# Taking the norms of one attention batch through a power operation on GpSimd, pair by pair, with its squares on ScalarE

## The chip, the cores and the metric

The kernel runs on one core of one Trainium2 chip. Times are device microseconds (us) of that core, medians of several executions. All runs told here were in the fast state but two: one of six runs of the last experiment was slow and is left out of its median, and one single run of the kernel before, told as such, has no state. Names: TensorE multiplies matrices, VectorE, ScalarE and GpSimd do elementwise work, SyncE issues most DMAs. In profile lines they are PE, DVE, ACT, POOL and SP. In these traces each engine works through its instructions in one fixed order, that of the program: both profiles of the changed kernel have TensorE's 4161 matmuls in the same order.

## The reference

Cosine attention for 8 batches of 12 heads (448 tokens, 64 numbers per head), then a two-layer feed-forward with a quick GELU.

```python
q_n = q / (np.linalg.norm(q, axis=-1, keepdims=True) + 1e-06)
k_n = k / (np.linalg.norm(k, axis=-1, keepdims=True) + 1e-06)
scores = np.matmul(q_n, k_n.transpose(0, 1, 3, 2)) / tau     # then softmax, then @ v
# ...
h = x @ w_in
g = h * (1.0 / (1.0 + np.exp(-1.702 * h)))
return (g @ w_out).astype(np.float32)
```

## The kernel before

Heads are handled in pairs; pairs 0 to 5 are batch 0, 6 to 11 batch 1, and so on. A planner inside the program simulates the engines with fixed durations and writes the instructions of each engine in the order that comes out, so a change of a planned duration also changes orders. For each pair: load q, k and v; square; sum per head and token; make the inverse norm; scale q and k to fp16 ("qks"); transpose them ("tps", copied out as "qkT"); scores ("sp"), exponential ("et"), times values, normalise. When a batch's heads are done, its first feed-forward product begins ("mm" from w_in, then tanh "th" and gate "gT"), later the second (w_out).

```python
SQP, SQT, XA, CA = range(HP, 2 * HP), (0, 1), (), (0, 1)   # HP = 6: squares of pairs 6..11 on GpSimd
...
def square(x, ti):
    ...
    if sq_pool(x, ti):
        return nc.gpsimd.tensor_tensor(out=sqs[x, ti], in0=src, in1=src, op=ALU.mult)
    return nc.scalar.activation(out=sqs[x, ti], in_=src, func=AF.Square)
...
def newton(grp, ca, cb):                      # 3 VectorE instructions; called twice
    a, y, t = nrms[grp]
    nc.vector.scalar_tensor_tensor(out=t, in0=y, scalar=-ca, in1=y, op0=ALU.mult, op1=ALU.mult)
    nc.vector.tensor_tensor(out=t, in0=t, in1=a, op=ALU.mult)
    nc.vector.scalar_tensor_tensor(out=y, in0=t, scalar=cb, in1=y, op0=ALU.add, op1=ALU.mult)
...
def root(grp):                                # batch 0 only, before the first tanh
    nc.scalar.activation(out=a, in_=a, func=AF.Ln)
    nc.scalar.activation(out=a, in_=a, func=AF.Exp, scale=0.5)
...
groups = [(x,) for x in range(HP)]                                     # batch 0: one pair at a time
groups += [tuple(range(g, g + 2)) for g in range(HP, HALF, 2)]         # batch 1: in twos
groups += [tuple(range(g, g + GRP)) for g in range(HALF, NPAIR, GRP)]  # the rest: in threes
```

The three PSUM buffers of TensorE's products are given back mostly by VectorE (those of the w_out products by ScalarE): a product waits until VectorE's gate or copy has emptied the buffer it needs. TensorE also does filler transposes of a constant until 50 us, so as not to stand idle.

## Time and profile before

| | kernel before |
|---|---|
| time, median of 4 (with the run beside the changed kernel) | 445.4 us (444.07 to 446.61) |
| profiled span | 441.8 us |
| busy: TensorE, VectorE, ScalarE, GpSimd | 426.5, 240.6, 302.6, 146.2 us |
| first product of batch 1 starts | 99.18 us |
| loads of batch 2 resume | 74.21 us |

The span is shorter than the time of the run by some 2 us of start and end. A start time in the table is read from the timeline, the first line of that kind.

### The profile page before, as it was taken

The numbers are of one execution on the slowest core, as the hardware profiler recorded it, in microseconds if no ns is written. First come the engines' busy times: TensorE is split into PE (matmuls) and PEld (weight loads), VectorE is DVE, ScalarE is ACT, GpSimd is POOL, SyncE is SP. The second block draws the span as 40 slices with busy tenths as digits, with TensorE's granted clock in tenths as the row PEclk, the third lists the DMA queues.
The fourth block names the chain that finished last, engine by engine and source line by source line (L and its number), as shares of the span: only waits on it lengthen the run. The fifth ranks groups of instructions, "written<-read, shape, count | busy, mean of one in ns | idle before, by whom it ended". The sixth has DMA issues, their size and how long they took to land.

```text
span 441.8 us, 10584 instructions
## 1 busy us (share of the span) xinstructions
PE 426.5 (97%) x4174; PEld 262.6 (59%) x4174; DVE 240.6 (54%) x629; ACT 302.6 (69%) x478; POOL 146.2 (33%) x209
## 2 busy tenths in 40 slices
PE   8899989989999998999999999999999999999995
PEld 8768876554555654566555655555556655565563
DVE  4767987795877668653675338641552115404400
ACT  5889368959999878866887678865776466314411
POOL 2745767276436663324060613333000000000000
PEclk9999999999999999999999999999999999999999
DMA  9999298999999999666555766644311130021022
GB/s 222 242 226 264 69 163 173 244 245 281 217 218 204 230 248 187 178 132 173 173 131 114 209 182 130 158 103 127 54 26 46 50 96 13 12 73 36 1 72 73
DMA packets 95889, 64.00 MB, mean 145 GB/s; under 512 B 56288, under 2 KB 90848, under 8 KB 95840
## 3 DMA queue, kind: packets, MB, share of 16 engines
q1 hardware_dynamic: 91952, 56.81, 55.3%
q0 software_dynamic: 3648, 6.29, 8.0%
q8 instruction: 33, 0.54, 0.5%
q10 hardware_dynamic: 240, 0.23, 0.1%
q14 instruction: 16, 0.13, 0.1%
HBM read 45.61 MB, written 11.01 MB: 128 GB/s over the span
## 4 chain that ended last, share of the span: by engine, by line
PE 84%; DVE 5%; ACT 4%; DMA 2%; POOL 2%; issue 1%; SPq 0%; POOLq 0%; ACTq 0%
PE mm L557 31%; PE mm L502 28%; PE sp L377 7%; PE avp L403 7%; PE tps L348 4%; PE mm L532 2%; ACT et L388 2%; DMA k<-in_k_dram 2%; PE mm L456 2%; PE sp L439 2%; POOL qks L316 2%; PE tps L340 1%; DVE n L250 1%; ACT sq L244 1%; DVE gT L544 1%
## 5 line engine op out<-in xcount | busy, mean ns | idle before, releaser
L388 ACT ACTIVATE et<-sp 112x896 f16<-112x896 f32 x192 | 166.7, 917 | 39.8 <-PE sp L377 33.4
L557 PE MATMUL mm<-w_out,gT 128*128 128x384 f16 x896 | 154.8, 326 | 0.4 <-DVE xT L489 0.4
L502 PE MATMUL mm<-xT,w_in 128*128 128x448 f16 x672 | 135.4, 353 | 1.4 <-DVE gT L519 1.3
L557 PEld LDWEIGHTS <-gT 128*128 128x128 f16 x896 | 83.8, 98 | 65.5 <-issue 13.8
L502 PEld LDWEIGHTS <-w_in 128*128 128x128 f16 x672 | 62.3, 98 | 68.8 <-issue 15.6
L519 DVE SCALAR_TENSOR_TENSOR gT<-th,mm 128x448 f16<-128x448 f16 x112 | 68.8, 617 | 60.7 <-ACT th L512 60.7
L512 ACT ACTIVATE th<-mm 128x448 f16<-128x448 f32 x128 | 69.8, 548 | 39.5 <-PE mm L502 28.7
L250 DVE TENSOR_REDUCE n<-sq 112x8 f32<-112x512 f32 x96 | 63.6, 678 | 28.8 <-ACT sq L244 28.1
L332 POOL CAST vt<-v 112x256 f16<-112x256 f32 x92 | 35.0, 404 | 114.1 <-PE avp L403 73.6
L316 POOL TENSOR_TENSOR qks<-k,y 112x512 f16<-112x512 f32 x42 | 43.8, 1043 | 40.0 <-DVE y L291 33.0
L568 ACT ACTIVATE ost<-mm 128x384 f32<-128x384 f32 x56 | 27.5, 491 | 42.9 <-PE mm L557 41.1
L403 PEld LDWEIGHTS <-et 112*128 112x128 f16 x1152 | 44.7, 97 | 11.3
L414 DVE RECIPROCAL rcx<-avp 128x4 f32<-128x4 f32 x72 | 13.0, 180 | 62.9 <-PE avp L403 62.4
L403 PE MATMUL avp<-vt,et 112*128 112x65 f16 x1152 | 46.7, 193 | 0.0
L316 POOL TENSOR_TENSOR qks<-q,y 112x512 f16<-112x512 f32 x42 | 43.8, 1043 | 0.0
L377 PE MATMUL sp<-qkT 64*128 64x448 f16 x288 | 41.1, 355 | 0.0
L244 ACT ACTIVATE sq<-k 112x512 f32<-112x512 f32 x42 | 26.4, 633 | 8.9 <-DMA k<-in_k_dram 7.0
L417 DVE TENSOR_TENSOR xf<-avp,rcx 128x256 f16<-128x256 f32 x72 | 30.6, 424 | 2.5
L244 ACT ACTIVATE sq<-q 112x512 f32<-112x512 f32 x42 | 26.3, 633 | 0.8 <-DVE n L250 0.4
L348 PE MATMUL tps<-ident 128*128 128x128 f16 x254 | 19.4, 238 | 3.2 <-DVE qkT L352 1.8
L348 PEld LDWEIGHTS <-ident 128*128 128x128 f16 x254 | 17.3, 108 | 4.7 <-issue 3.3
L532 PE MATMUL mm<-xT,w_in 128*128 128x224 f16 x192 | 20.0, 259 | 0.1
(44 smaller groups left out, 217.3 us busy)
## 6 DMA issues: line engine op xcount, KB each, us to landing
k<-in_k_dram SPq DMA_DIRECT2D x48, 224.0 KB, 4.5
v<-in_v_dram SPq DMA_DIRECT2D x48, 224.0 KB, 4.5
q<-in_q_dram SPq DMA_DIRECT2D x47, 224.0 KB, 4.6
w_in<-in_moe_w_in_dram POOLq DMA_DIRECT2D x2, 1536.0 KB, 16.3
w_out<-in_moe_w_out_dram POOLq DMA_DIRECT2D x2, 1536.0 KB, 11.1
out_dram<-ost SPq DMA_DIRECT2D x7, 336.0 KB, 2.9
out_dram<-ost SPq DMA_DIRECT2D x8, 288.0 KB, 3.2
out_dram<-ost SPq DMA_DIRECT2D x8, 240.0 KB, 3.0
```

Source lines behind the costliest of these rows:

```text
L244: return nc.scalar.activation(out=sqs[x, ti], in_=src, func=AF.Square)
L250: nc.vector.tensor_reduce(out=n2s[grp][:, x - grp[0], ti], in_=sqs.pop((x, ti)), axis=AX.X, op=ALU.add,)
L316: return eng.tensor_tensor(out=qkss[x][:, 1 - ti].rearrange("p c j d -> p j c d"), in0=src, in1=rss[x][:, ti, :, :, None].to_broadcast((P, ...
L332: copy(out=vt[:, :, j, :D], in_=src[:, j]) for j in range(2)
L348: nc.tensor.transpose(out=tps0[:, 2 * S : 2 * S + 128], in_=ident, identity=ident)
L377: nc.tensor.matmul(out=sp[:, j, :S], lhsT=keys(x, j, c), rhs=queries(x, j, 0, S), start=True, stop=True,)
L388: nc.scalar.activation(out=e[:, : 2 * S].rearrange("p (j s) -> p j s", j=2), in_=sps.pop(key)[:P, :, :S], func=AF.Exp, scale=inv_tau, **kw,)
L403: nc.tensor.matmul(out=ps[:, (D + 1) * t : (D + 1) * (t + 1)], lhsT=exps[x, c][:, q0 : q0 + 128], rhs=values(x, c, D * j, D * j + D + 1), ...
L502: nc.tensor.matmul(out=ps[:, :S], lhsT=w_in_sb[:, kk, 128 * m : 128 * (m + 1)], rhs=xTs[b, kk][:, :S], start=(kk == 0), stop=(kk == KT1 - 1),)
L512: nc.scalar.activation(out=ths[key], in_=mms[key][:, :S], func=AF.Tanh, scale=0.851)
L519: nc.vector.scalar_tensor_tensor(out=gts[b // 2][:, m, (b % 2) * S : (b % 2 + 1) * S], in0=ths.pop((b, m)), scalar=1.0, in1=mms.pop((b, m) ...
L557: nc.tensor.matmul(out=mms[b2, t, n][:, :NW], lhsT=gts[b2][:, kk, 128 * t : 128 * (t + 1)], rhs=w_out_sb[:, kk, NW * n : NW * (n + 1)], st ...
```

## The change

The norms of batch 1 are freed from VectorE. Their square root becomes one power (exponent 0.5) per pair on GpSimd, the twelve squares move to ScalarE, and the w_out loads are planned earlier.

```diff
-    SQP, SQT, XA, CA = range(HP, 2 * HP), (0, 1), (), (0, 1)
+    SQP, SQT, XA, CA, TA, POW = (), (0, 1), (), (0, 1), (), range(HP, 2 * HP)
...
+    root_of = const.tile([P, 1], FP32)          # filled with 0.5
...
+    def power(grp):
+        a = n2s[grp]
+        flat = a.rearrange("p g a b c -> p (g a b c)")
+        return nc.gpsimd.tensor_tensor(
+            out=flat, in0=flat, in1=root_of.to_broadcast((P, 16 * len(grp))), op=ALU.pow
+        )
...
-    groups += [tuple(range(g, g + 2)) for g in range(HP, HALF, 2)]
+    groups += [tuple(range(g, g + 1)) for g in range(HP, HALF)]
...
+        if x == grp[0] and x in POW:
+            add(("norm", 0, grp), "POOL", 0.4 + 2.3 * n, early + 0.3, partial(power, grp), after=reds)
+            add(("norm", 1, grp), "DVE", 0.45, early + 0.3, partial(inverse, grp), after=[("norm", 0, grp)])
...
-        add(("w_out", i), "POOL", 1.0, 9 + i, partial(load_w_out, i), ...
+        add(("w_out", i), "POOL", 1.0, 3 + i, partial(load_w_out, i), ...
```

In the first lines `POW` names the pairs whose norm is a power; `TA` is empty and does nothing here. The function `inverse` (an add of 1e-6 and a reciprocal on VectorE) was there already for batch 0.

More of the change, by code (lines that the diff above doesn't have):

```diff
@@ L351, in transposed @@
         qkTs[x] = p_qkT.tile([128, 2, S], FP16, name="qkT")
-        nc.vector.tensor_copy(out=qkTs[x], in_=tpss.pop(x))
+        (nc.scalar.copy if x in TA else nc.vector.tensor_copy)(out=qkTs[x], in_=tpss.pop(x))
     def dma_transposed(x):
@@ L641 @@
                 add(("norm", 1, grp), "DVE", 0.45, early + 0.3, partial(inverse, grp), after=[("norm", 0, grp)])
-        if x == grp[0] and not first:
+        if x == grp[0] and x in POW:
+            add(("norm", 0, grp), "POOL", 0.4 + 2.3 * n, early + 0.3, partial(power, grp), after=reds)
+            add(("norm", 1, grp), "DVE", 0.45, early + 0.3, partial(inverse, grp), after=[("norm", 0, grp)])
+        elif x == grp[0] and not first:
             add(("norm", 0, grp), "DVE", 0.78 + 0.06 * n, early + 0.3, partial(norm_a, grp), after=reds, **port)
@@ L652 @@
                 after=[("scale", 0, x), ("scale", 1, x)], takes=[("a", 1), ("qkT", 1)], frees=[("qks", 2)])
-            add(("qkT", x), "DVE", 0.6, s - 3, partial(transposed, x), after=[("tp", x)], frees=[("a", 1)])
+            add(("qkT", x), "ACT" if x in TA else "DVE", 0.8 if x in TA else 0.6, s - 3, partial(transposed, x), after=[("tp", x)], frees=[("a", 1)])
         else:
@@ L770 @@
             dma=packets(768, 4096), **port)
-        add(("w_out", i), "POOL", 1.0, 9 + i, partial(load_w_out, i), hold=[("load", "q", 2 * HP - 1)],
+        add(("w_out", i), "POOL", 1.0, 3 + i, partial(load_w_out, i), hold=[("load", "q", 2 * HP - 1)],
             dma=packets(1024, 3072), **port)
@@ L775 @@
     make_identity(nc, ident)
+    nc.vector.memset(root_of, 0.5)
     for vt in vts:
```

## The prediction

> **What bounds the kernel now.** I read four views in this order: the page, the busy time of each engine in stretches of ten microseconds, the timelines of VectorE and GpSimd between 30 and 110 us, and the waits. The page first:
>
> ```profile
> PE 426.5 (97%) x4174; PEld 262.6 (59%) x4174; DVE 240.6 (54%) x629; ACT 302.6 (69%) x478; POOL 146.2 (33%) x209
> ...
> PE   8899989989999998999999999999999999999995
> ...
> DVE  4767987795877668653675338641552115404400
> ACT  5889368959999878866887678865776466314411
> POOL 2745767276436663324060613333000000000000
> ```
>
> TensorE is busy in 97% of the span and full in nearly every slice after the ninth (a slice is 11 us). VectorE and GpSimd, whose work the change moves, are full nowhere but between about 40 and 70 us. That is where batch 1 is prepared: its norms, its scaled queries and keys, and the first scores, beside the first feed-forward product of batch 0. The stretches show it:
>
> ```profile
> 30.00:40.00 10.00, 9.57 (x162) 8.01 (x161) 5.65 (x17) 9.30 (x13) 3.08 (x3) 1.00 1.11 260
> 40.00:50.00 10.00, 8.90 (x125) 8.35 (x125) 9.53 (x24) 5.12 (x8) 8.08 (x12) 1.00 0.78 184
> 50.00:60.00 10.00, 9.28 (x106) 9.03 (x104) 9.25 (x22) 4.35 (x8) 6.83 (x9) 1.00 0.51 81
> 60.00:70.00 10.00, 9.10 (x131) 6.44 (x132) 8.53 (x25) 8.04 (x10) 6.97 (x7) 1.00 1.05 178
> 70.00:80.00 10.00, 9.28 (x145) 6.08 (x143) 6.19 (x21) 8.37 (x12) 4.75 (x6) 1.00 0.77 178
> 80.00:90.00 10.00, 8.60 (x123) 5.29 (x119) 8.67 (x28) 9.88 (x16) 2.78 (x7) 1.00 1.10 243
> ```
>
> After the stretch come TensorE, its weight loads, VectorE, ScalarE, GpSimd, the clock, the DMA share and GB/s. From 40 to 60 us VectorE is at 94% while ScalarE idles half the time, because no score of batch 1 exists yet; from 80 us ScalarE is full of the exponentials that came late. The VectorE timeline shows Newton steps standing still:
>
> ```profile
> 44.66 1.04 DVE L276 SCALAR_TENSOR_TENSOR t<-y 112x32 f32<-112x32 f32 x1
> ...
> 56.59 2.15 DVE L263 TENSOR_SCALAR y<-n 112x32 int32<-112x32 int32 x1
> ```
>
> and the GpSimd timeline names what ran beside them:
>
> ```profile
> 44.61 1.04 POOL L243 TENSOR_TENSOR sq<-k 112x512 f32<-112x512 f32 x1
> ...
> 56.66 1.04 POOL L316 TENSOR_TENSOR qks<-k,y 112x512 f16<-112x512 f32 x1
> 57.66 1.03 POOL L316 TENSOR_TENSOR qks<-q,y 112x512 f16<-112x512 f32 x1
> ```
>
> The same L276 takes 0.18 us at 51.92 when GpSimd is not on a tensor. The Newton work of pairs 6 and 7 starts at 44.45 and ends at 53.38: 8.9 us for some 2 us of arithmetic.
>
> **What the Trainium skill says.** (1) "SBUF — State Buffer" calls the second port pair of VectorE, shared with GpSimd, an exclusive lock: a VectorE instruction in a two-port mode, or with two SBUF inputs against a GpSimd instruction that reads SBUF, waits until the other is done (its list of key terms, "shared port pair"). The trace agrees: 1.04 against 0.18 us above. (2) "GPSIMD Engine Reference", section "Performance versus the Vector engine", gives 2.6 cycles per element for an add on GpSimd and nothing for a power; no run so far shows one. (3) "ScalarE: Activation LUTs", section "Table sets: the hidden batching unit", says that exp and ln share one set and exp and tanh another, so a logarithm between tanh calls would cost a table load. The trace has two loads of 1.283 us, one at the start and one before the first tanh; the instruction order of the changed kernel also has two. So batch 1, which lies among the tanh calls, could not take batch 0's root by logarithm and exponential for free; Square causes no load.
>
> **The change part by part.** (a) Removed from VectorE: three groups of two pairs, eleven instructions each. From the groups by shape: L263 3.0, L276 2.0, L279 1.3, L280 1.3, L287 0.5, L290 1.1, L291 0.6, together 9.8 us, of which about 3 us is waiting for the port. (b) Added to VectorE: an add and a reciprocal for each of six pairs. Batch 0's rows of the same shape measure 319 and 253 ns, so 6 x 0.57 = 3.4 us. VectorE loses 6.4 us net in 40 to 73 us. (c) Moved: twelve squares leave GpSimd (12 x 1.04 = 12.5 us) and go to ScalarE (12 x 0.633 = 7.6 us), into the hole that ScalarE has from 40 to 60 us (10.5 us idle). (d) Added to GpSimd: six powers on 112x16. No row has one. The kernel's own plan enters 2.7 us for it; I take that, because its other GpSimd figures hold (a scale planned at 1.0, spaced 1.00 us in the timeline; a cast planned at 0.75, measured 0.75). So 6 x 2.7 = 16.2 us: GpSimd gains 3.7 us net. (e) The norms come pair by pair, so batch 1's first transposes come earlier. Counting both TensorE orders: they stand after 180 of the 192 first-product matmuls before, after 96 of 192 in the changed kernel. Thirteen of 254 filler transposes go as well. (f) The second half of the w_out load follows the first at once, instead of 9.0 us later (53.69 and 62.69 before).
>
> What can be gained at most? From the pieces of the chain, one matmul of L532 takes 0.096 us, L557 0.163, L456 0.037, L439 0.075, L340 and L479 0.05, L502 0.19. Times the counts of each stretch, real TensorE work is 8.1, 8.8, 8.7, 9.1, 8.2 and 10.0 us in the six stretches from 40 to 100 us: 53 of 60. So the change has 7 us to win there, 1.6% of the time. After 100 us TensorE idles for 1.3 us once and never again before the end.
>
> How much of the 7? Following the new GpSimd order by hand: ScalarE gives the second square of pair 6 at about 39, VectorE its sum at 39.9, the first power ends at 42.6. A pair then costs one power, two scales and a share of casts, 2.7 + 2.0 + 0.4 = 5.1 us; with the two w_out issues at about 52 to 54 us (1.9 us), the last pair is scaled at about 72.8 and transposed by 73.2. In the kernel before, the last transposes of batch 1 end at 77.2 and batch 1's own first product starts at 99.3, 22.1 us later. Behind that point the changed order holds 92 L557, 96 L456, 28 L439 and 14 L479 matmuls: 15.0 + 3.5 + 2.1 + 0.7 = 21.3 us; with 1.5 us of stalls (2.5 us before) the first product of batch 1 starts at 96.0. That is **3.3 us earlier**. From there the order is nearly the old one, so I carry the 3.3 us to the end.
>
> **The rivals.** *GpSimd becomes the pace.* The six pairs cost it 5.1 us each, as much as TensorE has to do meanwhile; nothing measured stands behind 2.7 us. If a power takes 4 us, six of them add 7.8 us and the gain turns into a loss of about 4 us; at 1.7 us TensorE is the bound and the gain nears 5.5. *The port.* A power may hold the port for its 2.7 us and stop the next pair's add on VectorE, and with it the gates behind it; five such collisions at up to 2.7 us would give VectorE back its 6.4 us and leave about 0 to 1 us. For it: the collisions shown above. Against: VectorE is below 90% after the change. *The loads.* The waits of the queues have one large entry:
>
> ```profile
> SPq L231 <- DMA w_out<-in_moe_w_out_dram: 32.0, 1, 32.0
> ```
>
> Batch 2's loads wait for w_out until 74.2 us, and ScalarE then waits for keys at 150 to 166 us. If the data come no earlier, TensorE just waits where it now waits 1.3 us. Issuing the second half early hides nothing by itself, since the DMA engines were busy without a break between the halves; only the earlier first half (about 1.7 us) counts. Under this rival the gain is 1 to 2 us.
>
> **Range and chances.** I take 3.3 us off 446.3 us: 443.0 us. The range goes from the 7 us ceiling (439.5) to a slow power (447.5). Over 2% faster would need 8.9 us, more than the ceiling of 7: 3%. Over 2% slower needs a power of about 5 us or a broken order: 5%. Within 2%: 92%.
>
> **What would show it.** Right: powers spaced near 2.7 us; VectorE 6 us less busy in all; ScalarE at 7 to 8 tenths between 40 and 60 us; the first scores of batch 1 near 49 us instead of 60.5; its first product near 96 us. Wrong: TensorE waiting at the batch 1 transposes for GpSimd by more than 4 us in all; adds on VectorE lasting over 1 us beside powers; the first product of batch 1 early but a larger wait for keys by 170 us.

## The result

The changed kernel takes 439.62 us (439.36 to 440.5, 4 runs) against 445.4 us. The ratio is 0.9874, with a 95% interval of 0.9837 to 0.9912. A second set gave 439.57 us against 444.25 us, ratio 0.9885 (0.9862 to 0.9909). A ratio is the mean time of one kernel's fast runs over that of the other's of the same rounds, so not quite the ratio of the medians quoted. Executions over 1.5% slower than the fastest of the same kernel are left out of the means. The interval shows a real gain of 1.2 to 1.3%, about 5 us.

First the page of the changed kernel, engine totals and tenths per slice of 11 us:

```profile
PE 425.0 (97%) x4161; PEld 260.2 (59%) x4161; DVE 238.3 (54%) x612; ACT 307.3 (70%) x490; POOL 151.2 (34%) x203
...
PE   8898999999999999999999999999999999999996
...
DVE  4866987785876768643775339641552115404400
ACT  5889977859999878776797578765776466314411
POOL 2752998276437564333060604343100000000000
```

VectorE lost only 2.3 us of busy time (the prediction said 6), GpSimd gained 5.0, ScalarE 4.7. From 44 to 77 us the digits of GpSimd now read 9, 9, 8 where they read 7, 6, 7. The stretches of ten microseconds, with the same columns as in the prediction:

```profile
40.00:50.00 10.00, 9.74 (x140) 8.47 (x137) 9.41 (x20) 9.93 (x18) 9.28 (x7) 1.00 1.08 232
50.00:60.00 10.00, 9.06 (x128) 6.84 (x124) 9.67 (x25) 7.76 (x12) 9.99 (x8) 1.00 0.60 94
60.00:70.00 10.00, 10.00 (x142) 8.39 (x138) 7.03 (x15) 7.92 (x13) 10.00 (x8) 1.00 1.16 211
70.00:80.00 10.00, 9.76 (x172) 6.84 (x168) 8.00 (x24) 8.85 (x13) 6.08 (x12) 1.00 0.61 161
80.00:90.00 10.00, 9.01 (x92) 5.32 (x89) 8.16 (x26) 8.06 (x14) 3.69 (x8) 1.00 1.11 266
```

ScalarE's hole from 40 to 60 us is mostly gone (9.93 and 7.76 us busy in ten) and its crush at 80 us has eased (9.88 to 8.06). GpSimd has no gap from 41 to 74 us. VectorE is still nearly full from 40 to 60 us. The moved squares have a price, too: one that waited for its keys holds up the first tanh behind it (37.50 us instead of 36.46), and TensorE waits 1.40 us for the gate after that, at 38.75 us. VectorE's group of adds shows why its total fell so little; this is the groups by shape, with count, busy time and mean in ns:

```profile
L315 DVE TENSOR_SCALAR yv<-n 112x16 f32<-112x16 f32 x12 | 7.4, 615 | 1.3 <-POOL n L308 1.1
```

Six of the twelve are batch 0's, which took 319 ns on average in the kernel before. In the timeline of VectorE the six of batch 1 take 0.36, 1.00, 0.96, 0.78, 1.05 and 1.01 us, 0.86 on average. The timelines of GpSimd and of VectorE around one power say what holds them:

```profile
45.35 2.90 POOL L308 TENSOR_TENSOR n<-n,root_of 112x16 f32<-112x16 f32 x1
48.22 1.04 POOL L325 TENSOR_TENSOR qks<-q,yv 112x512 f16<-112x512 f32 x1
```

```profile
48.29 1.00 DVE L315 TENSOR_SCALAR yv<-n 112x16 f32<-112x16 f32 x1
```

The power ends at 48.25. That releases both the add on VectorE and the next instruction on GpSimd, and GpSimd's scale starts 0.07 us sooner. It has the port for its whole 1.04 us, so the add lasts 1.00 us. The Trainium skill ("SBUF — State Buffer", section "Terms") calls the port an exclusive lock; these lines agree. The lock is lost to the scale behind the power, not to the power.

Two more lines of the timelines give the position of TensorE at the first product of batch 1, before and after:

```profile
99.18 1.30 PE L502 MATMUL mm<-xT,w_in 128*128 128x448 f16 x6
```

```profile
96.75 2.43 PE L511 MATMUL mm<-xT,w_in 128*128 128x448 f16 x12
```

### The profile page after: what moved, and what is told of

It is laid out like the page before. It is cut to its first block, busy times and chain, and to the rows that moved or that the text cites. A ratio compares the mean times of both kernels' runs of the same rounds, so it can differ in the third digit from the quotient of the medians.

```text
span 438.5 us, 10541 instructions
## 1 busy us (share of the span) xinstructions
PE 425.0 (97%) x4161; PEld 260.2 (59%) x4161; DVE 238.3 (54%) x612; ACT 307.3 (70%) x490; POOL 151.2 (34%) x203
## 4 chain that ended last, share of the span: by engine, by line
PE 82%; POOL 5%; issue 4%; DVE 4%; DMA 2%; ACT 1%; SPq 0%; POOLq 0%; ACTq 0%; DVEq 0%
PE mm L566 33%; PE mm L511 28%; PE sp L386 8%; PE avp L412 8%; PE tps L357 3%; POOL n L308 3%; POOL qks L325 1%; DMA q<-in_q_dram 1%; DMA k<-in_k_dram 1%; DVE n L251 1%; ACT et L397 1%; PE mm L465 1%; PE sp L448 1%; PE tps L349 1%; DVE yv L315 1%
## 5 line engine op out<-in xcount | busy, mean ns | idle before, releaser
L325 POOL TENSOR_TENSOR qks<-k,y 112x512 f16<-112x512 f32 x36 | 37.5, 1043 | 31.4 <-DVE y L292 23.2
L325 POOL TENSOR_TENSOR qks<-q,y 112x512 f16<-112x512 f32 x36 | 37.5, 1043 | 0.0
L245 ACT ACTIVATE sq<-k 112x512 f32<-112x512 f32 x48 | 30.4, 636 | 7.8 <-DMA k<-in_k_dram 6.4
L245 ACT ACTIVATE sq<-q 112x512 f32<-112x512 f32 x48 | 30.5, 638 | 3.3 <-DMA q<-in_q_dram 2.1
L541 PE MATMUL mm<-xT,w_in 128*128 128x224 f16 x192 | 21.0, 259 | 1.6 <-DVE gT L553 1.6
L308 POOL TENSOR_TENSOR n<-n,root_of 112x16 f32<-112x16 f32 x6 | 17.4, 2902 | 12.5 <-DVE n L251 12.5
L357 PE MATMUL tps<-ident 128*128 128x128 f16 x241 | 18.3, 235 | 3.2 <-DVE qkT L361 1.8
```

The source lines that it names most:

```text
L325: return eng.tensor_tensor(out=qkss[x][:, 1 - ti].rearrange("p c j d -> p j c d"), in0=src, in1=rss[x][:, ti, :, :, None].to_broadcast((P, ...
L357: nc.tensor.transpose(out=tps0[:, 2 * S : 2 * S + 128], in_=ident, identity=ident)
```

## The experiments

All twelve kernels gave correct results. Each ratio is to the kernel before, run on the same chip in the same set; `...` in a diff marks a cut.

### The change alone, repeated

> The changed kernel, unaltered, once more, as the measure for the runs beside it. The record says 439.6 us against 445.4, 1.3% less, while the two profiled spans differ by only 3.3 us (441.8 and 438.5). If the profiled execution of the kernel before was one of its quick ones, this run has again a ratio near 0.987 and the kernel before spreads by 2 us or more. If 3.3 us is the true gain, the ratio is near 0.9925.

439.57 us, ratio 0.9885: the first number was no accident. The span of this profile is 437.8 us and its first product of batch 1 starts at 95.87 us.

### The kernel before, repeated

> The kernel before, for a second profile beside its first of 441.8 us span. Its runs spread from 443.1 to 446.6 us. If its profile was one of the quick ones, this one shows a span of 442 to 444 us and more waiting of TensorE between 45 and 100 us; the end after 200 us should be the same to 0.2 us.

445.22 us (the other runs of the same kernel in that set: median 444.46), span 443.4 us. The first profile was indeed a quick one. I expected the extra time before 100 us, and that was wrong: the first product of batch 1 starts at 99.39 us, only 0.2 later than in the first profile. Most of the extra 1.6 us (1.4) comes after it. These are the stretches of the two profiles of the kernel before, this one second:

```profile
160.00:170.00 10.00, 9.91 (x84) 5.32 (x82) 5.12 (x12) 7.85 (x14) 5.49 (x7) 1.00 0.96 223
170.00:180.00 10.00, 8.69 (x82) 4.84 (x81) 8.05 (x23) 7.90 (x14) 7.08 (x9) 1.00 0.89 136
```

```profile
160.00:170.00 10.00, 9.57 (x82) 5.23 (x81) 4.69 (x11) 7.40 (x13) 6.56 (x8) 1.00 1.00 209
170.00:180.00 10.00, 8.60 (x74) 4.60 (x73) 9.15 (x26) 8.47 (x15) 5.85 (x8) 1.00 1.02 166
```

So there is a second place where TensorE waits, at 150 to 180 us, while the DMA engines are full, and it varies from run to run. From 100 to 200 us TensorE idles 1.40 and 2.27 us in the two profiles of the kernel before, 1.05 and 1.10 us in those of the changed kernel.

That splits the gain of the profiles. Up to the first product of batch 1: 99.18 and 99.39 against 96.75 and 95.87, on average 3.0 us. From there to the block of 96 second-product matmuls near the end (it starts at 382.42, 384.01, 379.44 and 378.61): on average 283.9 against 282.7, that is 1.2 us. From the start of that block all four take 59.1 to 59.4 us.

### The squares alone

```diff
 # kernel before
-    SQP, SQT, XA, CA = range(HP, 2 * HP), (0, 1), (), (0, 1)
+    SQP, SQT, XA, CA = (), (0, 1), (), (0, 1)
```

> The kernel before with one part of the change: its twelve squares of batch 1 on ScalarE. Newton steps in twos stay on VectorE, w_out stays late. Its TensorE order has batch 1's first transposes after 96 of 192 first-product matmuls, as the changed kernel. If moving the squares is what pays (they open GpSimd and so the port), it reaches about 441. If the power is needed to free VectorE, VectorE stays at its limit from 40 to 60 us and the time is 444 to 446.

441.59 us against 444.25 us, ratio 0.9936 (0.9909 to 0.9962): 2.7 us, about half of the gain, without any power. The groups of its Newton steps in twos show the port set free:

```profile
L276 DVE SCALAR_TENSOR_TENSOR t<-y 112x32 f32<-112x32 f32 x6 | 1.1, 191 | 0.2
L263 DVE TENSOR_SCALAR y<-n 112x32 int32<-112x32 int32 x3 | 0.5, 175 | 0.0
```

In the kernel before these rows have means of 330 and 999 ns. Nothing else was edited, so it was the squares on GpSimd, and where they put the scales in its order, that VectorE stood behind.

That the freed port is what brought the 2.7 us is not shown, though. In this profile (440.1 us, 1.7 less than the first of the kernel before) TensorE is not ahead at the first product of batch 1: it starts at 101.05 us instead of 99.18, behind 8 more scores and 13 more filler transposes, some 1.3 us by the costs in the prediction (8 x 0.075 + 13 x 0.05). The gain comes later. The same two stretches as above have no wait at all, and from 100 to 200 us TensorE idles 0.0 us (1.40 and 2.27 in the kernel before):

```profile
160.00:170.00 10.00, 10.00 (x85) 5.49 (x84) 5.68 (x15) 8.51 (x14) 0.41 (x1) 1.00 1.06 260
170.00:180.00 10.00, 10.00 (x97) 5.47 (x96) 8.30 (x22) 8.51 (x15) 7.46 (x10) 1.00 0.63 121
```

With the squares gone GpSimd also issues both halves of w_out in one go, though they were planned late:

```profile
52.83 1.82 POOL L599 DMA_DIRECT2D w_out<-in_moe_w_out_dram  x2
```

In the kernel before they left at 53.69 and 62.69 us. Batch 2's loads resume at 71.70 us, 2.5 us earlier, and from 75 to 200 us ScalarE waits 1.2 us for keys and queries instead of 4.7. So the rival of the loads fits this part of the gain better than the port does; no run here separates the two.

### Everything but the power

```diff
 # changed kernel
-    SQP, SQT, XA, CA, TA, POW = (), (0, 1), (), (0, 1), (), range(HP, 2 * HP)
+    SQP, SQT, XA, CA, TA, POW = (), (0, 1), (), (0, 1), (), ()
```

> The changed kernel with the power taken out: pair by pair, squares on ScalarE, w_out early, but each pair's norm by Newton steps on VectorE. The plan puts the first transposes of batch 1 even earlier, after 60 of 192 matmuls. If the power is what pays, VectorE has 66 small instructions in place of 12, waits at the port, and the time is 442 to 446. If pairs and squares pay and the power does not, 438 to 440.

446.51 us, ratio 1.0041: slower than the kernel before, and 6.9 us slower than the changed kernel of the same set. Taking the norms pair by pair is a loss as long as Newton steps do it in the order that this plan makes (TensorE's order changed as well: first transposes after 60 matmuls and not 96), for 60 small instructions then go through VectorE (ten a group; the prediction's eleven and the 66 above were a miscount). The port does not enter (each step takes 0.17 to 0.18 us, the reciprocal 0.25); the order of VectorE's work does. Its timeline at the worst place, first and last of a row of 16 Newton instructions, and the copy that comes after them:

```profile
60.26 0.17 DVE L277 SCALAR_TENSOR_TENSOR t<-y 112x16 f32<-112x16 f32 x1
...
63.42 0.17 DVE L292 TENSOR_TENSOR y<-y,t 112x16 f32<-112x16 f32 x1
63.52 0.27 DVE L498 COPY xT<-mm 128x224 f16<-128x224 f16 x1
```

The product that waited for this copy of 0.27 us, in TensorE's timeline:

```profile
63.84 2.40 PE L541 MATMUL mm<-xT,w_in 128*128 128x224 f16 x12 [2.79 <-DVE xT L498]
```

Twelve such matmuls take 1.31 us elsewhere. Here they take 2.40, because the wait of 2.79 us cost the clock too. The granted clock is the third number from the end:

```profile
61.00:62.00 1.00, 0.04 (x2) 0.00 (x0) 0.86 (x6) 0.30 (x1) 0.00 (x0) 1.00 1.16 210
62.00:63.00 1.00, 0.00 (x0) 0.00 (x0) 0.83 (x6) 0.00 (x0) 0.00 (x0) 0.65 1.15 209
63.00:64.00 1.00, 0.16 (x2) 0.12 (x2) 0.93 (x5) 0.00 (x0) 0.23 (x1) 0.50 1.17 214
```

It stays at 0.50 until 69 us at least. The 0.65 puts the fall between 62 and 63 us, less than 2 us after TensorE's last work at 61.05. The Trainium skill describes this ("TensorE: Matmul & The Clock Gate", "Part 1: The HAM clock gate"): the clock falls to half after an idle window that the page puts at about 3.4 us. Here it fell during a wait of 2.79 us.

### The w_out loads

```diff
 # changed kernel
-        add(("w_out", i), "POOL", 1.0, 3 + i, ...
+        add(("w_out", i), "POOL", 1.0, 9 + i, ...
```

> The changed kernel with the w_out load planned where it was before. TensorE's order is exactly that of the changed kernel. My theory (early transposes of batch 1 bring the gain, the load order little): within 1 us of the changed kernel, about 440. The rival that the earlier w_out and the loads of batch 2 behind it bring the gain: 2 to 4 us slower, 442 to 444.

440.55 us, ratio 0.9912 against 0.9885 for the changed kernel beside it: about 1 us, with intervals that overlap (0.9887 to 0.9936 and 0.9862 to 0.9909). But the two w_out issues stand at 53.06 us in both traces, both in one go, and batch 2's loads resume at 72.28 and 72.19 us. What the edit did was to place a few other instructions differently (I had written that TensorE's order was the same; only its counts were, and line by line it differs). So planning w_out earlier did not make it earlier, and this run does not test the rival of the loads: w_out was early here too, because the squares were gone from GpSimd. What the 1 us comes from stays open.

### Powers for two pairs at once

```diff
 # changed kernel
-    groups += [tuple(range(g, g + 1)) for g in range(HP, HALF)]
+    groups += [tuple(range(g, g + 2)) for g in range(HP, HALF, 2)]
```

> The changed kernel with its powers taken for two pairs at once (three of 32 wide in place of six of 16). If a power costs by the element, GpSimd spends the same 17 us, one power takes about 5.6 us, and the first pair of batch 1 waits for the second: first transposes after 168 of 192 matmuls by the plan, and the time goes back to 443 to 445. If a power has a large fixed cost, the row shows 3 to 4 us each and GpSimd gets 6 us back; then about 440.

443.81 us, ratio 0.9989: all of the gain is gone. The group of the power in this run:

```profile
L308 POOL TENSOR_TENSOR n<-n,root_of 112x32 f32<-112x32 f32 x3 | 16.3, 5433 | 3.1 <-DVE n L251 3.1
```

5.43 us for 32 numbers per partition and 2.90 for 16: by the line through both, 0.158 us per number and 0.37 us fixed. So splitting costs nearly nothing, and going pair by pair lets the first pair start sooner: batch 1's first real transposes begin at 48.69 us in the changed kernel, and at 58.40 us here. Newton steps in twos, in the squares alone above, had a ratio of 0.9936: in twos the power is slower than they are. It pays only pair by pair.

### Each power done twice

```diff
 # changed kernel, in power()
+        idle = p_n.tile([P, 16 * len(grp)], FP32, name="idle")
+        nc.gpsimd.tensor_tensor(out=idle, in0=flat, in1=root_of.to_broadcast(...), op=ALU.pow)
```

> The changed kernel with each power done a second time into an unused tile, so GpSimd has 6 x 2.9 = 17.4 us more between 40 and 75 us; the plan is not told and the orders stay. If GpSimd paces that stretch, TensorE waits at the transposes, last transposes near 91 us, and the time grows by 10 us or more, to 450 to 455. If it has slack, by less than 5 us.

457.46 us, ratio 1.0300. Six extra powers of 2.90 us are 17.4 us; the time is 17.9 us above the changed kernel's 439.57 of the other set. GpSimd has hardly any slack in this stretch: with more to do, it paces batch 1 (the last transposes end at 91.15 us instead of 74.38). The clock falls again, with stretches of 0.69 to 0.97 between 40 and 90 us, so the agreement of 17.4 and 17.9 is partly luck.

### The squares left on GpSimd

```diff
 # changed kernel
-    SQP, ... = (), ...
+    SQP, ... = range(HP, 2 * HP), ...
```

> The changed kernel with its twelve squares left on GpSimd: powers alone. GpSimd then has 12.4 us more on top of a stretch in which it has no gap. By the slope of the doubled powers (17.4 us more work, 17.9 us more time) this costs some 8 to 12 us: 448 to 452, slower than the kernel before. If the squares find room before 41 us, where GpSimd idles for 12 us, it costs 3 us or less.

447.75 us, ratio 1.0075 (1.0036 to 1.0115): slower than the kernel before, by a little less than expected. The power pays only with the squares gone from GpSimd.

### Powers for the first two pairs only

```diff
 # changed kernel
-    SQP, SQT, XA, CA, TA, POW = (), (0, 1), (), (0, 1), (), range(HP, 2 * HP)
+    SQP, SQT, XA, CA, TA, POW = (), (0, 1), (), (0, 1), (), range(HP, HP + 2)
...
-    groups += [tuple(range(g, g + 1)) for g in range(HP, HALF)]
+    groups += [(HP,), (HP + 1,)] + [tuple(range(g, g + 2)) for g in range(HP + 2, HALF, 2)]
```

> The changed kernel with the power for the first two pairs of batch 1 alone; the other four go in twos by Newton steps, whose port is free now that the squares are on ScalarE. GpSimd loses 4 x 2.9 = 11.6 us from 53 us on. If GpSimd's pace holds batch 1 up, the last transposes end near 70 us in place of 74 and the time is 436.5 to 438.5. If VectorE's queue is what matters, the blocks of 11 Newton steps stop the copies behind them and it is 440 to 443.

443.37 us, ratio 0.9968. Freeing GpSimd of 11.6 us did not pay; the second branch of the expectation held, with a time a little above its range. TensorE's longest wait, in its timeline:

```profile
63.58 1.31 PE L541 MATMUL mm<-xT,w_in 128*128 128x224 f16 x12 [2.23 <-DVE gT L553]
```

VectorE's timeline has Newton steps for pairs 10 and 11 in front of that gate, and two of them stand still:

```profile
60.79 0.98 DVE L277 SCALAR_TENSOR_TENSOR t<-y 112x32 f32<-112x32 f32 x1
61.80 0.96 DVE L280 TENSOR_TENSOR t<-t,n 112x32 f32<-112x32 f32 x1
...
62.91 0.61 DVE L553 SCALAR_TENSOR_TENSOR gT<-th,mm 128x448 f16<-128x448 f16 x1
```

GpSimd's timeline has two scales beside them:

```profile
60.68 1.03 POOL L325 TENSOR_TENSOR qks<-k,y 112x512 f16<-112x512 f32 x1
61.68 1.03 POOL L325 TENSOR_TENSOR qks<-q,y 112x512 f16<-112x512 f32 x1
```

The same two steps take 0.19 us each at 55.24 and 55.47 us, when GpSimd is not on a tensor. So the port was not free, as I had expected it to be: the squares had left it, the scales had not. Four small steps, two of them held at the port, stand before a gate, and TensorE waits 2.23 us for that gate, whose tanh was done at 61.23 us.

### The inverse norm straight from the power

```diff
 # changed kernel: exponent -0.5, no add and reciprocal on VectorE; the scales read the power's output
-    nc.vector.memset(root_of, 0.5)
+    nc.vector.memset(root_of, -0.5)
```

> The changed kernel with exponent -0.5, so that the power gives the inverse norm itself (the 1e-6 beside a norm near 0.8 is dropped, far under the tolerance) and the scales follow on GpSimd without VectorE's add and reciprocal. VectorE loses 6 x (0.96 + 0.25) us, of which 0.6 each was the wait for the port. If VectorE's queue still holds TensorE up in the changed kernel, 437 to 438.5; if GpSimd's pace alone decides, the same within 0.5 us, since GpSimd had no gap to lose.

446.05 us, ratio 1.0021: a miss. I had overlooked the buffers. The sums of squares now live until the scales have read them, and there are three buffers. VectorE's timeline:

```profile
59.72 0.69 DVE L251 TENSOR_REDUCE n<-sq 112x8 f32<-112x512 f32 x1 [4.11 <-POOL qks L327]
```

The sum for a later pair waits 4.11 us for GpSimd's scale to give a buffer back, everything behind it in VectorE's queue waits along, and TensorE's clock falls (0.83 of full from 50 to 60 us).

```diff
 # the same, mended
+    p_pw = pool("p_pw", 6)          # six buffers for batch 1's sums
```

> The exponent -0.5 again, with six buffers for the sums of squares. In the first try the powers wrote over the sums in place and the scales read them there, so VectorE's sum for a later pair had to wait 1.8 and 4.1 us for GpSimd to give back one of three buffers, and TensorE waited 4.4 us behind it. If that was the whole loss, this run is at or under the changed kernel's 439.6 (437.5 to 439.6). If it is 443 or more, the direct form has another fault.

440.38 us, ratio 0.9911 against the 0.9885 of the changed kernel in an earlier set. The fault was the buffers, but the form gains nothing over the changed kernel. It does move TensorE forward: the first product of batch 1 starts at 94.90 us. The lead is then lost. TensorE's timeline:

```profile
167.03 1.30 PE L514 MATMUL mm<-xT,w_in 128*128 128x448 f16 x6 [1.96 <-DVE gT L531]
```

Its waits after 100 us sum to 2.6 us (1.0 in the changed kernel), and ScalarE, which feeds the gates, waits 6.6 us for keys and queries from 75 to 200 us (3.1 in the changed kernel).

```diff
 # and on top: the first two pairs of batch 2 load without waiting for w_out
-        hold = ... [("w_out", 1)] if x == 2 * HP else []
+        hold = ... [("w_out", 1)] if x == 2 * HP + 2 else []
```

> The exponent -0.5 with its buffers, and one thing more: the loads of the first two pairs of batch 2 no longer wait for w_out, so that they use the hole in the DMA engines between 47 and 53 us. With the buffers alone the first product of batch 1 started at 94.9 us, a microsecond or two earlier than in the changed kernel, yet the end came no earlier: ScalarE waited 6.6 us for keys and queries and TensorE 2.6 us behind it at 167 to 172 us. If the loads set that limit, TensorE's wait after 100 us falls under 1 us and the time to 437 to 438.5. If something else holds TensorE there, it stays at 439.5 to 440.5. If the late w_out hurts the second product, TensorE waits for it at 65 to 80 us and it is over 441.

441.05 us, the median of five fast runs (438.85 to 443.12; a sixth, of 445.46, was slow), ratio 0.9924: no gain, and the test is not clean. The loads left at 61 us and not at 47, behind a load of values in the same queue that left only at 60.63 us. ScalarE's wait for the loads fell to 2.7 us and TensorE's wait behind the gates from 2.6 to 1.9 us, but other waits grew before 90 us. That the loads set the limit at 160 to 175 us is thus likely and not shown.

No kernel of these beats the changed one.

## Why the prediction was right, step by step

The time fell into the range. The gain was put at 3.3 us and is about 5. The time is at the low edge of the range, 0.1 us inside it (439.5). Some of that is the start: the prediction took its 3.3 us off 446.3 us, the median of three earlier runs, and the result has 445.4 us.

- **(a) Removal from VectorE, (c) squares.** The rows were right, but for the count of ten instructions a group. The squares alone bring 2.7 us, and I had not given them a number of their own. In their profile that gain lies after 100 us, beside earlier loads, and not in the preparation of batch 1 where I looked for it.
- **(b) The added adds and reciprocals.** Too small: 6 x 0.57 was 6 x (0.86 + 0.25) = 6.7 us, since five of the six adds lost the port to the scale. With 9.8 us of Newton steps gone that leaves 3.1 us; the total fell by 2.3 us and not by 6, the rest lying in rows of other batches (the first Newton step of the later ones went from 197 to 260 ns). VectorE stayed at 94 and 97% from 40 to 60 us, where I had it below 90%. My port rival blamed the power and five collisions of 2.7 us; it was the scale, at about 0.6 us of waiting in each of five. Two adds lasted over 1 us (1.05 and 1.01), which I had named as a sign of being wrong; TensorE waited little behind them.
- **(d) The power.** 2.90 us against the 2.7 taken from the plan. GpSimd's last scale ended at 73.95 us (72.8), the last transposes at 74.4 (73.2), and TensorE waited 0.3 us for GpSimd at batch 1's transposes (limit set: 4).
- **(e) Earlier transposes.** Right in kind: first scores of batch 1 at 50.7 us (49). I miscounted the order before: the first transposes stand after 168 of 192 matmuls, not 180.
- **(f) Loads.** Batch 2's loads resume at 72.19 us, 2.0 us earlier (1.7), but not for my reason. The first half of w_out left only 0.6 us earlier (53.06 us for 53.69), so the rest fits the second half, which follows at once: in the kernel before the DMA engines did slacken between the halves (86 GB/s from 64 to 66 us, 205 and 212 in the next two stretches of 2 us).
- **First product of batch 1.** 96.75 and 95.87 us in two profiles (96.0), so 3.0 us earlier on average. That this came so close to 3.3 is partly luck: the last transposes ended 1.2 and 0.8 us later than I had put them, and from there to the first product it took 22.4 and 21.8 us, not my 22.8.
- **The term that was mis-sized** is the last one, "I carry the 3.3 us to the end". In the profiles 1.2 us is won after that point as well, in the waits at 150 to 180 us. My rival of the loads took them as a limit on the gain; they came 2 us earlier, the waits shrank, and the gain grew. The 4.2 us of two profiles against two (4.4 by their spans) and the 5 us of the timed medians differ by what a spread of 2 us per kernel allows.

What stands shown: the squares by themselves are worth 2.7 us; pairs with Newton steps lose; the power is worth 6.9 us over Newton steps taken pair by pair, but the changed kernel is only 2.0 us faster than the best kernel with Newton steps, the squares alone; more work for GpSimd in the stretch costs time; two pairs per power give the gain back. What is argued: by which path the squares pay, the port or the earlier loads; that TensorE's remaining waits at 160 to 175 us are set by the loads.

## What to carry to other kernels

A small operation on a full in-order engine costs what waits behind it, not what it takes itself: sixteen steps of 0.2 us held up a copy of 0.27 us, and TensorE waited 2.79 us for it, while six operations of 2.9 us on GpSimd made TensorE wait 0.3 us for it at batch 1's transposes. When work moves off a shared port, look at what else its engine can now issue earlier: here, with the squares alone, batch 2's loads came 2.5 us sooner though nothing of theirs was edited. And see where in the trace the time is won before you name the cause. When a long operation is split, check that its cost is per element, and when a result is kept in place, count its buffers again.

## What the Trainium skill lacked or had wrong

- "GPSIMD Engine Reference" has no figure for a power. Here: 2.90 us for 112x16 and 5.43 us for 112x32 fp32, so 0.158 us per number and 0.37 us fixed.
- "SBUF — State Buffer" describes the lock and its winner as whoever starts first. It lacks a consequence that these runs show: an instruction on VectorE that waits for one on GpSimd becomes ready together with GpSimd's next one and can lose to it (0.78 to 1.05 us in five of six adds, in four of them right behind the power; 0.32 to 0.37 on average for batch 0's).
- "TensorE: Matmul & The Clock Gate" gives an idle window of about 3.4 us before the clock is halved. Here it was halved during a wait of 2.79 us, less than 2 us after TensorE's last work, and stayed so until 69 us at least, some 5 us after work had begun again.
